# Where the operands of the MLP matmuls start within 256 bytes: padding the tiles of x, h and the last weights

## The chip, the cores and the metric

The kernel runs on one core of a Trainium2 chip. The metric is the time of one execution on the device in microseconds (us), the median of several runs. In the names below TensorE is PE (its loading of a stationary operand is PEld), VectorE is DVE, ScalarE is ACT, GpSimd is POOL, and SyncE, which issues the DMAs, is SP.

## What is computed

Attention with mixed heads, then two MLPs one after the other, all in float32:

```
# q, k, v: (4, 12, 448, 64); w_pre, w_post: (12, 12)
scores = einsum('bhij,hg->bgij', scale * q @ k.T, w_pre)
attn   = softmax(scores);  attn = einsum('bhij,hg->bgij', attn, w_post)
x      = (attn @ v) as (1792, 768)
# two MLPs, 768 -> 2048 -> 768 each
h = x @ w_in;   g = where(h > 0, h, exp(min(h, 0)) - 1);  x   = g @ w_out
h = x @ w2_in;  r = maximum(h, 0);                        out = (r * r) @ w2_out
```

## The kernel before

The first 434 us are the attention, the rest the two MLPs; in the MLPs the 1792 tokens are taken in two halves of 896, and each half runs through four layers (w1i, w1o, w2i, w2o) one after the other.

Every product of the MLPs is made of three matmuls in a lower-precision float form: each operand is split into a high part (a copy rounded to that form) and a low part (what is left over), and `three` adds high by high, high by low and low by high into one PSUM bank. So each call of `three` is one matmul of line 587, one of line 588 and one of line 589, in this order, and the MLPs are a chain of these triples: 192 for each of the first three layers of a half, 224 for the last. All instructions stand in the order in which the code is written.

A matmul has a stationary operand (128 columns of it are loaded into the array, by a LDWEIGHTS that the trace shows as PEld) and a moving one, which is then streamed through. In the calls of `three` the second argument pair names the stationary parts and the third the moving ones.

- In the layers w1i, w1o and w2i the weights stand (`wh`, `wl`, 128 columns each time) and the activations move: 448 tokens of `xh`, `xl` (layers w1i, w2i) or of `hh`, `hl` (layer w1o).
- In the layer w2o it is the other way round: the activations stand (`hh`, `hl`, 128 tokens) and the weights move (`wh`, `wl`, 384 columns), since the output is to have tokens as rows.

The tiles: `two_parts` makes a high and a low tile for x (6 x 896 floats a partition) or h (16 x 896), in the right (`xp`) or left (`hp`) pool, with some room behind or ahead of the data. `Weights.part` makes the tiles `wh` and `wl` of 512 floats, of which 384 or 512 are used; those of the layer w2o, which has 384, begin `OFF` floats into the tile. The names `two_parts`, `OFF`, `hp` and `xp` carry the change. Which address a tile gets follows from the sizes of the tiles allocated before it in its pool.

Ahead of the matmuls ACT and DVE split weights and activations (lines 475 and 476, 628 and 629, 658 and 659), apply the activation functions (620 to 625), and in the first half also turn the weights from the words in which they come into float32.

Of the kernel before, what the change touches and what calls it, by code (L numbers as in the profile page):

```python
# [8 lines left out]
F32R = mybir.dt.float32r  # L9
# [11 lines left out]
JC, NJ = 4, 112  # L21
KC, FC = DM // 128, DFF // 128
WU = 512
OFF = 8
EXP_MIN, EXP_MAX = 2.0**-15, float.fromhex("0x1.dffffep+16")


# [373 lines left out]
class Weights:  # L401
# [64 lines left out]
    def part(self, engine=None):  # L466
# [4 lines left out]
        n = self.units[i][3]  # L471
        at = OFF * self.units[i][4]
        hi = self.pool.tile([128, WU], F32R, name="wh", bufs=4)[:, at : at + n]
# [31 lines left out]
def col(i):  # L505
    return slice(i * 128, (i + 1) * 128)


class Mlps:
# [17 lines left out]
    def two_parts(self, k, pool, name, at):  # L527

        n = k * 2 * S
        t = [pool.tile([128, n + 2 * OFF], F32R, name=f"{name}{a}", tag=f"{name}{a}") for a in "hl"]  # L530
        return [x[:, at : at + n].rearrange("p (k s) -> p k s", k=k) for x in t]


# [31 lines left out]
    def new_x(self, half):  # L565
        self.half, self.xraw = half, {}
        self.nx = self.two_parts(KC, self.xp, "x", OFF)

# [39 lines left out]
    def run(self):  # L608
        nc, weights, blocks = self.nc, self.weights, self.blocks
        self.hp = self.pool("hp", "left")  # L610
        for half in range(2):
            xh, xl = self.nx
            for m in range(2):
                hh, hl = self.two_parts(FC, self.hp, "h", m * OFF)
                pending = []

                def activate(p, f, bl, m=m, hh=hh, hl=hl):
                    u = g = self.tmp()
                    if m == 0:
                        nc.scalar.activation(u, p, AF.Relu, scale=-1.0)  # L620
                        nc.scalar.activation(u, u, AF.Exp, scale=-1.0)
                        nc.vector.scalar_tensor_tensor(g, u, -1.0, p, ALU.add, ALU.max)
                    else:
                        nc.scalar.activation(u, p, AF.Relu)  # L624
                        nc.vector.tensor_tensor(g, u, u, ALU.mult)  # L625

                    def rest():
                        nc.scalar.copy(hh[:, f, bl], g)
                        nc.vector.tensor_tensor(hl[:, f, bl], g, hh[:, f, bl].bitcast(F32), ALU.subtract)  # L629

                    pending.append(rest)

                def flush():
                    for rest in pending:
                        rest()
                    pending.clear()

                for f in range(FC):
                    if half == m == f == 0:
                        p = self.begun  # L640
                    else:
                        p = self.inner(xh, xl, flush)
                    for j, bl in enumerate(blocks):
                        activate(p[j], f, bl)
                flush()
                if m == 0:
                    xh, xl = self.two_parts(KC, self.xp, "x", OFF)
                    for o in range(KC):
                        p = [self.bank()[:, :S] for _ in blocks]
                        for f4 in range(4):  # L650
                            wh, wl = weights.next()
                            for j, bl in enumerate(blocks):
                                for i in range(4):
                                    f = 4 * f4 + i
                                    self.three(p[j], wh[:, col(i)], wl[:, col(i)], hh[:, f, bl], hl[:, f, bl],
                                               f == 0, f == FC - 1)
                        for j, bl in enumerate(blocks):
                            nc.scalar.copy(xh[:, o, bl], p[j])
                            nc.vector.tensor_tensor(xl[:, o, bl], p[j], xh[:, o, bl].bitcast(F32), ALU.subtract)
                    continue  # L660
                n2 = DM // 2
                for nh in range(2):
                    p = [self.bank()[:, :n2] for _ in range(7)]
                    for f in range(FC):
                        if half == 0 and nh == 0:
                            if f == 0:
                                self.new_x(1)
                            if f < 12:
                                self.load_x(f)
                            if 2 <= f < 14:  # L670
                                self.split_x(f - 2)
                        wh, wl = weights.next()
                        for i in range(7):
                            self.three(p[i], hh[:, f, col(i)], hl[:, f, col(i)], wh[:, :n2], wl[:, :n2],
                                       f == 0, f == FC - 1)
                    for i in range(7):
                        o = self.tmp()[:, :n2]
                        if i % 2:
                            nc.scalar.copy(o, p[i])
                        else:  # L680
                            nc.vector.tensor_copy(o, p[i])
                        r = half * 2 * S + i * 128
                        nc.sync.dma_start(out=self.out[r : r + 128, nh * n2 : (nh + 1) * n2], in_=o)
# [49 lines left out]
```

## Time and profile before

| | |
|---|---|
| median of 3 runs | 1380.01 us (1379.79 to 1380.43) |
| the profiled execution | 1380.93 us |
| its span, first to last instruction | 1379.2 us |
| PE, share of the span | 99% |
| DVE, ACT, POOL | 62%, 49%, 19% |
| mean granted TensorE clock | 0.998 |
| attention / MLPs, from the start | 0 to 434 us / 434 to 1379 us |

The span is what the trace covers; 1.7 us of the profiled execution's time lie around it. Matmuls are pipelined: one starts while the one before is still on its way through the array, so the duration of one matmul in the trace is longer than the distance from its start to the start of the next, and the ends are modelled. The distance between starts is what adds up to time.

### The profile page before, as it was taken

To read this page: it belongs to the slowest core of one execution; us is meant where nothing else is said; L and a number is where in the kernel's file an instruction comes from. 1 tells how busy PE (TensorE), PEld (TensorE's weight loads), DVE (VectorE), ACT (ScalarE), POOL (GpSimd) and SP (SyncE) were. 2 spreads that over 40 slices of the span, in tenths; PEclk is the share of its full clock that TensorE was granted. 3 is DMA by queue.
4 is the path that set the end of the run, shared out by engine and by line. 5 is a ranking of instruction groups with operands and counts; after the bars stand their busy time and mean duration, and the time that the engine had idled before them with its cause. 6 is when DMAs were issued, how large, how long until landed. Compare 5 with 4: busy or idle time off the path is not lost.

```text
span 1379.2 us, 24203 instructions
## 1 busy us (share of the span) xinstructions
PE 1368.0 (99%) x8908; PEld 1248.8 (91%) x8908; DVE 860.7 (62%) x1928; ACT 669.1 (49%) x1502; POOL 265.3 (19%) x247
## 2 busy tenths in 40 slices
PE   7999999999999999999999999999999999999998
PEld 5888888888888999999999999999999999999998
DVE  6877778777886999866699996634442113443121
ACT  5776767776766677422355543235541113333111
POOL 3765655674656000000000000000000000000000
PEclk9999999999999999999999999999999999999999
DMA  5633633733644655545355575532121111211131
GB/s 157 200 107 126 204 106 124 206 120 117 199 141 127 197 172 172 187 153 175 125 162 163 170 253 179 175 99 58 52 79 54 47 46 46 58 52 58 41 109 40
DMA packets 104842, 174.40 MB, mean 126 GB/s; under 512 B 22707, under 2 KB 82195, under 8 KB 104723
## 3 DMA queue, kind: packets, MB, share of 16 engines
q1 hardware_dynamic: 104723, 172.85, 39.9%
q8 instruction: 70, 1.15, 0.4%
q14 instruction: 49, 0.40, 0.1%
HBM read 97.93 MB, written 36.18 MB: 97 GB/s over the span
## 4 chain that ended last, share of the span: by engine, by line
PE 97%; DVE 1%; issue 0%; DMA 0%; SPq 0%; POOL 0%; ACT 0%; ACTq 0%; DVEq 0%; POOLq 0%
PE ps_post L221 12%; PE ps_qk L588 11%; PE ps_qk L589 11%; PE ps_qk L587 11%; PE ps_qk L246 6%; PE ps_mix L588 6%; PE ps_post L588 6%; PE ps_mix L589 6%; PE ps_post L589 6%; PE ps_mix L587 6%; PE ps_post L587 6%; PE ps_qk L163 4%; PE ps_mix L192 3%; PE ps_mix L190 3%; PE ps_mix L191 2%
## 5 line engine op out<-in xcount | busy, mean ns | idle before, releaser
L475 ACT CAST wh<-wf 128x384 fp32r<-128x384 f32 (+1 forms) x240 | 126.7, 532 | 267.5 <-DVE wf L461 116.1
L476 DVE TENSOR_TENSOR wl<-wf,wh 128x384 fp32r<-128x384 f32 (+1 forms) x238 | 137.5, 581 | 156.3 <-ACT wh L475 155.3
L184 POOL TENSOR_TENSOR gl<-graw,gh 120x448 fp32r<-120x448 f32 x178 | 201.3, 1152 | 146.2 <-ACT gh L179 140.8
L221 PEld LDWEIGHTS ps_post<-wg,ex 120*112 120x112 f32 x1440 | 156.1, 177 | 22.0 <-DVE tot L205 7.5
L221 PE MATMUL ps_post<-wg,ex 120*112 120x120 f32 x1440 | 173.0, 273 | 0.8 <-DVE at L228 0.6
L199 ACT ACTIVATE ex<-ps_mix,nmax 120x448 f32<-120x448 f32 x180 | 113.3, 637 | 113.3 <-DVE nmax L197 109.9
L588 PE MATMUL ps_qk<-xl,wh 128*128 128x448 f32 x384 | 141.0, 367 | 0.0
L589 PE MATMUL ps_qk<-xh,wl 128*128 128x448 f32 x384 | 140.7, 367 | 0.0
L587 PE MATMUL ps_qk<-xh,wh 128*128 128x448 f32 x384 | 139.4, 363 | 0.0
L197 DVE TENSOR_REDUCE nmax<-ps_mix 120x1 f32<-120x448 f32 x180 | 109.7, 622 | 42.3 <-PE ps_mix L192 41.8
L228 DVE COPY at<-ps_post 112x480 f32<-112x480 f32 x162 | 105.5, 651 | 10.0 <-PE ps_post L221 10.0
L179 ACT CAST gh<-graw 120x448 fp32r<-120x448 f32 x180 | 95.4, 593 | 1.7 <-DMA graw<-sc 1.7
L166 ACT COPY sc<-ps_qk 120x448 f32<-120x448 f32 x179 | 82.5, 557 | 8.1 <-PE ps_qk L163 8.1
L625 DVE TENSOR_TENSOR tmp<-tmp 128x448 f32<-128x448 f32 x64 | 39.9, 624 | 73.6 <-ACT tmp L624 73.6
L246 PEld LDWEIGHTS ps_qk<-at,v 112*64 112x64 f32 x1536 | 73.9, 137 | 11.3 <-ACT gh L179 6.2
L246 PE MATMUL ps_qk<-at,v 112*64 112x110 f32 (+2 forms) x1536 | 81.8, 262 | 0.0
L437 ACT ACTIVATE wf<-wd 128x384 f32<-128x384 f32 (+1 forms) x120 | 69.6, 580 | 17.9 <-DMA wd<-w1i 9.2
L587 PEld LDWEIGHTS ps_qk<-xh,wh 128*128 128x128 f32 x384 | 72.4, 188 | 6.4
L588 PEld LDWEIGHTS ps_qk<-xl,wh 128*128 128x128 f32 x384 | 72.0, 188 | 6.2
L589 PEld LDWEIGHTS ps_qk<-xh,wl 128*128 128x128 f32 x384 | 72.0, 188 | 5.2
L587 PE MATMUL ps_qk<-wh,hh 128*128 128x384 f32 x224 | 75.4, 336 | 0.0
L629 DVE TENSOR_TENSOR hl<-tmp,hh 128x448 fp32r<-128x448 f32 x128 | 74.2, 620 | 1.9 <-DMA w1if<-wf 1.5
(139 smaller groups left out, 3160.3 us busy)
## 6 DMA issues: line engine op xcount, KB each, us to landing
graw<-sc SPq DMA_DIRECT2D x180, 210.0 KB
wd<-w1i SPq DMA_DIRECT2D x32, 384.0 KB
wd<-w1o SPq DMA_DIRECT2D x24, 512.0 KB
wd<-w2i SPq DMA_DIRECT2D x32, 384.0 KB
wd<-w2o SPq DMA_DIRECT2D x32, 384.0 KB
w1if<-wf SPq DMA_DIRECT2D x32, 192.0 KB
w1of<-wf SPq DMA_DIRECT2D x24, 256.0 KB
w2if<-wf SPq DMA_DIRECT2D x32, 192.0 KB
```

Of the source, the lines that this page charges most:

```text
L179: nc.scalar.copy(hi, graw[t])
L184: engine.tensor_tensor(lo, graw.pop(t), parts[t][0].bitcast(F32), ALU.subtract)
L197: nc.vector.tensor_reduce(nmax, p, AX.X, ALU.max, negate=True)
L199: nc.scalar.activation(e[-1], p, AF.Exp, bias=nmax, scale=1.0, accum_out=tot[:, t % 2 : t % 2 + 1])
L221: nc.tensor.matmul(p[:, c, :], e[:, c * NJ : (c + 1) * NJ], w, start=True, stop=True)
L228: nc.vector.tensor_copy(o, p)
L246: nc.tensor.matmul(p[64 * a : 64 * a + 64, k, :w], vt[b, i][:, jc, g * D : (g + 1) * D], at[n][:, jc, 6 * i + g, :w], start=(jc == 0), sto ...
L475: nc.scalar.copy(hi, f)
L476: (engine or nc.vector).tensor_tensor(lo, f, hi.bitcast(F32), ALU.subtract)
L587: mm(p, wh, xh, start=first, stop=False)
L588: mm(p, wh, xl, start=False, stop=False)
L589: mm(p, wl, xh, start=False, stop=last)
```

## The change

Three things are changed in where data lie inside their tiles, nothing else. The constant `OFF` goes from 8 floats (32 bytes) to 40 (160 bytes); a second constant `STAND` of 24 floats (96 bytes) is used for the h tiles of the second MLP, which stand; and the room in each tile of x and h goes from 16 floats to 64, 192 bytes a tile more.

```
-OFF = 8
+OFF, STAND = 40, 24
...
     def two_parts(self, k, pool, name, at):
 
         n = k * 2 * S
-        t = [pool.tile([128, n + 2 * OFF], F32R, name=f"{name}{a}", tag=f"{name}{a}") for a in "hl"]
+        t = [pool.tile([128, n + 64], F32R, name=f"{name}{a}", tag=f"{name}{a}") for a in "hl"]
         return [x[:, at : at + n].rearrange("p (k s) -> p k s", k=k) for x in t]
...
             for m in range(2):
-                hh, hl = self.two_parts(FC, self.hp, "h", m * OFF)
+                hh, hl = self.two_parts(FC, self.hp, "h", m * STAND)
```

The constant `OFF` also stands in `new_x` and `run` (the x tiles) and in `Weights.part` (the tiles of w2o); these lines are not edited, but move with it. The addresses that the two built programs hold, as bytes past a multiple of 256, are the same for every matmul of a layer, because the operands step by 512 bytes (stationary) and 1792 or 1536 bytes (moving), all multiples of 256:

| layers | operand | before | now |
|---|---|---|---|
| w1i, w2i | moving `xh` / `xl` | 128 / 192 | 128 / 128 |
| w1o | moving `hh` / `hl` | 128 / 192 | 128 / 128 |
| w1i, w1o, w2i | stationary `wh`, `wl` | 96 | 224 |
| w2o | moving `wh`, `wl` | 128 | 128 |
| w2o | stationary `hh` / `hl` | 160 / 224 | 224 / 224 |
| MLPs | raw and temporary tiles `wd`, `wf`, `tmp` | 96 | 224 |

The tiles of the attention keep their addresses: among its 448-column matmuls, those of lines 190 to 192 have `gh` and `gl` moving at 192 and `pre_h` and `pre_l` standing at 96 and 64. On every engine the instructions of the two programs are the same and stand in the same order.

## Rows read from the trace of the kernel before

**Rows 1.** The page's busy shares, clock by slice and the chain by engine:

```profile
PE 1368.0 (99%) x8908; PEld 1248.8 (91%) x8908; DVE 860.7 (62%) x1928; ACT 669.1 (49%) x1502; POOL 265.3 (19%) x247
PEclk9999999999999999999999999999999999999999
PE 97%; DVE 1%; issue 0%; DMA 0%; SPq 0%; POOL 0%; ACT 0%; ACTq 0%; DVEq 0%; POOLq 0%
```

**Rows 2.** Busy time by stretch: attention, then layers of both halves.

```profile
core 0: us, PE busy (x) PEld busy (x) DVE busy (x) ACT busy (x) POOL busy (x), PEclk, DMA share, GB/s
0.00:434.00 434.00, 426.36 (x4003) 361.43 (x4004) 340.19 (x906) 304.51 (x776) 262.09 (x244) 0.99 0.48 149
435.00:556.00 121.00, 121.00 (x670) 111.74 (x669) 107.41 (x223) 78.97 (x158) 2.26 (x3) 1.00 0.56 177
557.00:673.00 116.00, 116.00 (x573) 107.15 (x572) 76.57 (x137) 35.67 (x63) 0.00 (x0) 1.00 0.51 164
674.00:790.00 116.00, 116.00 (x572) 107.17 (x571) 104.22 (x220) 60.53 (x126) 0.00 (x0) 1.00 0.50 157
791.00:906.00 115.00, 115.00 (x665) 114.98 (x664) 80.21 (x170) 39.66 (x79) 0.00 (x0) 1.00 0.58 186
...
1025.00:1141.00 116.00, 116.00 (x572) 107.18 (x571) 23.90 (x38) 21.42 (x39) 0.00 (x0) 1.00 0.17 50
```

**Rows 3.** Line 587's matmuls, layer w1o of each half: duration, first and last start.

```profile
engine op xcount: duration ns min/median/max, first and last start us, forms
L587 PE MATMUL ps_qk<-hh,wh x96: 361/363/364, 576.4 to 673.4; 128*128 128x448 f32 x96
L587 PE MATMUL ps_mix<-hh,wh x48: 362/362/364, 556.9 to 651.4; 128*128 128x448 f32 x48
...
L587 PE MATMUL ps_qk<-hh,wh x96: 361/363/364, 1024.7 to 1121.7; 128*128 128x448 f32 x96
...
L587 PE MATMUL ps_post<-hh,wh x48: 362/363/364, 1046.7 to 1141.3; 128*128 128x448 f32 x48
```

**Rows 4.** The same for line 587 in layer w2o, first half.

```profile
L587 PE MATMUL ps_mix<-wh,hh x64: 335/336/340, 791.1 to 906.6; 128*128 128x384 f32 x64
L587 PE MATMUL ps_post<-wh,hh x64: 335/336/337, 791.7 to 907.1; 128*128 128x384 f32 x64
```

**Rows 5.** PE's timeline in layer w1o: start, duration, both us.

```profile
599.58 0.36 PE L587 MATMUL ps_post<-hh,wh 128*128 128x448 f32 x1
599.78 0.37 PE L588 MATMUL ps_post<-hl,wh 128*128 128x448 f32 x1
599.99 0.37 PE L589 MATMUL ps_post<-hh,wl 128*128 128x448 f32 x1
600.19 0.36 PE L587 MATMUL ps_post<-hh,wh 128*128 128x448 f32 x1
```

**Rows 6.** Groups by line and shape over the span: busy us, mean ns of one.

```profile
L588 PE MATMUL ps_qk<-xl,wh 128*128 128x448 f32 x384 | 141.0, 367 | 0.0
L589 PE MATMUL ps_qk<-xh,wl 128*128 128x448 f32 x384 | 140.7, 367 | 0.0
L587 PE MATMUL ps_qk<-xh,wh 128*128 128x448 f32 x384 | 139.4, 363 | 0.0
L587 PE MATMUL ps_qk<-wh,hh 128*128 128x384 f32 x224 | 75.4, 336 | 0.0
L588 PE MATMUL ps_qk<-wl,hh 128*128 128x384 f32 x224 | 75.4, 336 | 0.0
L589 PE MATMUL ps_qk<-wh,hl 128*128 128x384 f32 x224 | 75.4, 336 | 0.0
```

**Rows 7.** The attention's 448-column mix matmuls: three of a timeline, then durations.

```profile
301.69 0.36 PE L190 MATMUL ps_mix<-gh,pre_l 120*120 120x448 f32 x1
301.89 0.36 PE L191 MATMUL ps_mix<-gh,pre_h 120*120 120x448 f32 x1
302.09 0.37 PE L192 MATMUL ps_mix<-gl,pre_h 120*120 120x448 f32 x1
...
L191 PE MATMUL ps_mix<-gh,pre_h x180: 358/363/576, 20.5 to 428.1; 120*120 120x448 f32 x180
L192 PE MATMUL ps_mix<-gl,pre_h x180: 362/367/575, 21.5 to 428.3; 120*120 120x448 f32 x180
```

**Rows 8.** The end of the program: last matmul, last eviction, all stores.

```profile
1375.30 0.34 PE L589 MATMUL ps_qk<-wh,hl 128*128 128x384 f32 x1
1375.73 0.56 DVE L681 COPY tmp<-ps_qk 128x384 f32<-128x384 f32 x1 [0.54 <-PE ps_qk L589]
...
L683 SPq DMA_DIRECT2D out<-tmp x28: 332/338/2063, 847.0 to 1376.3; - x28
```

## Prediction, written before the changed kernel ran

> **What bounds the kernel now.** I began with the page's busy shares and the chain of what ended last. PE is busy for 99% of the span, the chain runs through PE for 97% of it, and nothing else has more than 1%; the clock row is at its top in all 40 slices, the 2.4 GHz level [rows 1]. So the time is the sum of what the matmuls take, one after the other, and a change counts only if it alters the distance from one matmul's start to the next.
>
> Next come the stretches. In the MLP layers PE is busy for the whole of each stretch (116.00 of 116 us), while DVE is busy for 24 to 107 us and ACT for 21 to 79 [rows 2]. No layer waits for an operand. The pace is then read from the first and last start of line 587, which opens each triple. In layer w1o of the first half the first of its 192 starts is at 556.9 and the last at 673.4: 116.5 / 191 = 0.610 us a triple, 203.3 ns a matmul. In the second half it is 1024.7 to 1141.3, 116.6 us [rows 3], the same within the rounding of these rows. In layer w2o the 224 starts go from 791.1 to 907.1: 116.0 / 223 = 0.520 us a triple, 173.4 ns a matmul [rows 4].
>
> What should they take? The two shapes differ by 64 columns, and line 587's durations differ by 363 - 336 = 27 ns [rows 6], which is 64 columns at one a cycle of 2.4 GHz (26.7 ns). So streaming alone is 448 / 2.4 = 186.7 ns and 384 / 2.4 = 160.0 ns. What is left over per matmul is **16.6 ns in the 448-column layers and 13.4 ns in w2o**. These layers run the same triple, with the same number of columns loaded (128). The surplus differs by 3.2 ns, and the durations say where it lies. Lines 588 and 589 take 367 ns where 587 takes 363, in the 448-column layers alone; in w2o all three take 336 [rows 6].
>
> Three things can make this difference: the other engines' traffic, the number of columns, or where operands start. The first is out. Layer w1o of the first half runs beside 76.6 us of DVE, 35.7 us of ACT and a DMA share of 0.51, and that of the second half beside 23.9, 21.4 and 0.17 [rows 2], at the same pace. Nor can it be that 587 reloads the stationary part that 588 then uses, while the others change it: in w2o the triple repeats its stationary part in the same way, and there the lines are equal. Between columns and starts the profile doesn't decide by itself. The starts do differ: w2o moves everything from 128 and has its stationary parts at 160 and 224, while the other layers move from 128 and 192 with stationary parts at 96.
>
> **The change, part by part.** No instruction is added, removed or moved on any engine, so there are no new waits, and no queue is reordered. What is new are addresses.
>
> *Layers w1i, w1o, w2i.* There are 6 such layers of 576 matmuls, 3456 or 1152 triples. Low parts move from 128 instead of 192, and weights stand at 224 instead of 96. That brings them to a pair of starts that w2o holds already: there line 588 streams weights from 128 while `hl`, standing at 224, is loaded for line 589, and it takes 336 ns like its neighbours. I price this from two sides:
> - By durations: if 588 and 589 come down to 587's 363 ns, that is 2 x 4 ns x 1152 = 9.2 us.
> - By surplus: if the layers come to w2o's 13.4 ns, that is 3.2 ns x 3456 = 11.1 us.
>
> I take the middle, **10.1 us**. A lower price comes from the attention's mix matmuls, also 448 columns wide, with both parts alike (at 192) and stationary ones at 96 and 64. They start 0.20 us apart, 0.60 us a triple [rows 7] against 0.61 in w1o [rows 5]. With only two decimals that says somewhere from 0 to 10 ns a triple, 0 to 11.5 us. They load 120 columns instead of 128 and run beside a busier POOL, so I use them as a bound only. The other bound is the shortest record among them, 358 ns: if every 448-column matmul came to that, the gain would be (5 + 9 + 9) x 1152 = 26 us.
>
> *Layer w2o.* Its moving start stays at 128, and the high stationary part goes from 160 to 224, where the low one is. Lines 587 to 589 have equal durations although their stationary starts differ [rows 6], so I put it at 0. The bounds: 5 ns better, which is the gap from 363 to the 358 of the mix, or 4 ns worse, the step that 588 and 589 show elsewhere, both times 1344 matmuls: -6.7 to +5.4 us.
>
> *The other engines.* `wd`, `wf` and `tmp` shift by 128 bytes modulo 256, so the splitting on ACT and DVE and the DMAs read and write at other starts. No row shows that this matters to them, and I take 0. What covers it is room: in the fullest layer DVE has 107.4 us of work in 121, in the next 104.2 in 116 [rows 2]. A matmul stream 1.5% faster shortens 116 us to 114 and still leaves DVE 10 us. Without that cover, DVE would have to become 10% slower before PE waits for splits.
>
> *Attention and tail.* The first 434 us keep their addresses; the end, from the last matmul at 1375.3 over the last copy to the last store issued at 1376.3 and its landing [rows 8], is untouched. Both 0.
>
> The sum: 1380.93 us of the profiled execution less 10.1 is 1370.8. That execution lay 0.9 us above the median of 1380.01, so the median to expect is **1370 us**, 0.7% faster.
>
> The Trainium skill speaks against this. "TensorE: Matmul & The Clock Gate", section "Step-by-step: what each phase is for", says that PE has two independent read ports into SBUF, so that loading the next stationary operand takes nothing from the matmul that is streaming. By that rule starts could not matter, and the time would stay at 1380. The same page's section "Back-to-back issue gap" gives columns / 2.4 + 2.5 ns for an isolated warm matmul, as an estimate 189.2 and 162.5 ns here. The trace shows 203.3 and 173.4, so here each matmul pays about 11 to 14 ns that this formula doesn't hold, and the measurement decides.
>
> **The rivals.**
> - *No change (about 1380).* The 3.2 ns belong to the number of columns, or to the pattern of accumulating into one bank, and starts do nothing. For it: no row names an address, and 587 already does 363 ns while moving from 128, the start from which 589 is slow. Against it: nothing else differs inside a triple of the 448-column layers that doesn't also differ in w2o, and there the lines are equal. If surplus merely grew with columns, w2o's 13.4 would become 15.6 at 448, leaving 1.0 ns x 3456 = 3.5 us for starts, a time of 1376.5. Chance 0.17 for within 0.2%, about what a measurement of this kernel can tell from no change (1377.2 to 1382.8).
> - *Slower (about 1387).* A moving start of 128 against a stationary start of 224 is itself a bad pair over 448 columns. Line 589 shows that 128 alone doesn't protect: it moves from 128 and takes 367. Then line 587 goes from 363 to 367 (4 ns x 1152 = 4.6 us), 588 and 589 keep theirs, and w2o, now at 224 for all, pays up to half of its bound of 5.4: 1380 + 4.6 + 2.7 = 1387. It decides from a mean of 0.8 ns a matmul over the 3456 (2.8 us). Against it stands w2o's line 588, which has this pair and shows nothing. Chance 0.13.
> - *Much faster (1355 to 1361).* All lines reach the 358 ns of the shortest mix record: 1380 - 26 = 1354. Only some of those records are that short (the median of line 191 is 363), so it is a tail. Chance 0.07.
> - *Half of it (1374).* Only the low part's move to 128 counts and only line 588 comes down: 4 ns x 1152 = 4.6 us, 1375.4; or only 589 does, the same. Chance 0.14.
>
> **How the numbers follow.** The forecast itself, both slow lines down to the third (1366 to 1374), has 0.49. With half of it and much faster that makes 0.70 for faster by over 0.2%, 0.17 for the same, 0.13 for slower. The likeliest case's own range is 1366 to 1374. To leave out no more than 2 in 10, the range cuts off most of the slower case (0.13) and much faster (0.07) and keeps no change: 1361 to 1382.
>
> **What would show it.** If the forecast is right, lines 588 and 589 of the 448-column layers read about 363 ns, the first and last start of 587 in layer w1o lie 114.6 to 115.0 us apart instead of 116.5, w2o keeps 116.0, and the attention's end stays at 434 us. It is wrong in its mechanism if 588 and 589 stay at 367 while time falls elsewhere, for example in w2o or on line 587, and wrong altogether if all durations stay. It would also be wrong if PE shows idle time in the MLPs, which it doesn't now.

## The result, and the profile after

The changed kernel takes 1368.26 us (median of 4 runs, 1367.12 to 1369.38) against 1380.1 us: a ratio of 0.9915, 95% interval 0.9904 to 0.9927, 0.85% faster. The profiled execution took 1367.75 us with a span of 1366.0, and its clock was 0.998 as before.

The busy shares of the page after, then the busy time by stretch, with the columns of [rows 2]:

```profile
PE 1355.9 (99%) x8908; PEld 1247.1 (91%) x8908; DVE 859.9 (63%) x1928; ACT 668.6 (49%) x1502; POOL 265.3 (19%) x247
...
0.00:432.00 432.00, 425.48 (x4002) 360.24 (x4003) 339.96 (x906) 304.29 (x775) 261.95 (x244) 1.00 0.48 150
554.00:668.00 114.00, 114.00 (x572) 106.98 (x571) 76.03 (x137) 35.13 (x63) 0.00 (x0) 1.00 0.51 166
669.00:783.00 114.00, 114.00 (x572) 106.98 (x571) 104.38 (x220) 60.20 (x126) 0.00 (x0) 1.00 0.52 160
1016.00:1130.00 114.00, 114.00 (x572) 106.98 (x570) 23.88 (x38) 21.11 (x39) 0.00 (x0) 1.00 0.17 51
```

PE is still never idle in the MLPs, and the work of the other engines is the same to within 1 us over the span. Only the distance between matmuls is new. Line 587's matmuls after, in layer w1o of both halves and in w2o of the first (duration min/median/max, first and last start, as in [rows 3, 4]), and one group each of lines 588 and 589 in w1o:

```profile
L587 PE MATMUL ps_qk<-hh,wh x96: 362/362/363, 572.5 to 667.9; 128*128 128x448 f32 x96
L587 PE MATMUL ps_mix<-hh,wh x48: 362/362/363, 553.3 to 646.3; 128*128 128x448 f32 x48
...
L587 PE MATMUL ps_qk<-hh,wh x96: 362/362/363, 1015.4 to 1110.8; 128*128 128x448 f32 x96
L587 PE MATMUL ps_post<-hh,wh x48: 362/362/363, 1037.0 to 1130.0; 128*128 128x448 f32 x48
...
L587 PE MATMUL ps_mix<-wh,hh x64: 335/336/336, 783.7 to 899.2; 128*128 128x384 f32 x64
L587 PE MATMUL ps_post<-wh,hh x64: 336/336/336, 784.2 to 899.7; 128*128 128x384 f32 x64
...
L588 PE MATMUL ps_qk<-hl,wh x96: 362/362/363, 572.7 to 668.1; 128*128 128x448 f32 x96
L589 PE MATMUL ps_qk<-hh,wl x96: 362/362/363, 572.9 to 668.3; 128*128 128x448 f32 x96
```

Layer w1o now goes from 553.3 to 667.9: 114.6 / 191 = 0.600 us a triple, 200.0 ns a matmul, against 203.3 of [rows 3], and all three lines have the same duration, which before they had not [rows 6]. Layer w2o keeps its 116.0 us and 173.4 ns. So each 448-column matmul now has the 13.3 ns above streaming that w2o had before.

The first triple of the MLPs starts at 432.8 in this profile and the last at 1361.8; the MLPs' matmuls take 929.3 us against 940.6 before, 11.3 us less, and the two medians lie 11.8 us apart. The span fell by 13.2, because the MLPs also began 1.9 us earlier (432.8 against 434.7). That looks like scatter between executions and not like the change: in the profiles of the eleven experiments below, where the attention is again the same, they began between 433.0 and 434.5.

One place in the profile after doesn't fit the idea of a pair of starts with one pace. PE's timeline after, in the first triples of the MLPs and then after the attention's last value matmuls, which stand behind the first 36:

```profile
433.72 0.37 PE L588 MATMUL ps_mix<-xl,wh 128*128 128x448 f32 x1
433.92 0.37 PE L589 MATMUL ps_mix<-xh,wl 128*128 128x448 f32 x1
434.13 0.37 PE L587 MATMUL ps_mix<-xh,wh 128*128 128x448 f32 x1
434.34 0.37 PE L588 MATMUL ps_mix<-xl,wh 128*128 128x448 f32 x1
...
445.92 0.36 PE L587 MATMUL ps_qk<-xh,wh 128*128 128x448 f32 x1
446.12 0.36 PE L588 MATMUL ps_qk<-xl,wh 128*128 128x448 f32 x1
446.32 0.36 PE L589 MATMUL ps_qk<-xh,wl 128*128 128x448 f32 x1
```

The same tiles at the same starts run at 207 ns apart first (433.72 to 434.34 is three steps) and at 200 later. The experiments had to explain this too.

### The profile page after: what moved, and what is told of

It is laid out like the page before. It is cut to its first block, busy times and chain, and to the rows that moved or that the text cites. A ratio compares the mean times of both kernels' runs of the same rounds, so it can differ in the third digit from the quotient of the medians.

```text
span 1366.0 us, 24203 instructions
## 1 busy us (share of the span) xinstructions
PE 1355.9 (99%) x8908; PEld 1247.1 (91%) x8908; DVE 859.9 (63%) x1928; ACT 668.6 (49%) x1502; POOL 265.3 (19%) x247
## 4 chain that ended last, share of the span: by engine, by line
PE 97%; DVE 1%; issue 0%; SPq 0%; DMA 0%; POOL 0%; ACT 0%; ACTq 0%; DVEq 0%; POOLq 0%
PE ps_post L221 12%; PE ps_qk L587 11%; PE ps_qk L588 11%; PE ps_qk L589 11%; PE ps_qk L246 6%; PE ps_mix L587 6%; PE ps_post L587 6%; PE ps_post L588 6%; PE ps_mix L589 6%; PE ps_mix L588 6%; PE ps_post L589 6%; PE ps_qk L163 4%; PE ps_mix L192 3%; PE ps_mix L190 3%; PE ps_mix L191 3%
## 5 line engine op out<-in xcount | busy, mean ns | idle before, releaser
L246 PEld LDWEIGHTS ps_qk<-at,v 112*64 112x64 f32 x1536 | 73.8, 137 | 11.3 <-ACT gh L179 6.5
L589 PE MATMUL ps_qk<-wh,hl 128*128 128x384 f32 x224 | 75.3, 336 | 0.0
L588 PE MATMUL ps_qk<-wl,hh 128*128 128x384 f32 x224 | 75.3, 336 | 0.0
```

What stands on the lines that cost most here:

```text
L246: nc.tensor.matmul(p[64 * a : 64 * a + 64, k, :w], vt[b, i][:, jc, g * D : (g + 1) * D], at[n][:, jc, 6 * i + g, :w], start=(jc == 0), sto ...
L588: mm(p, wh, xl, start=False, stop=False)
L589: mm(p, wl, xh, start=False, stop=last)
```

## The experiments

All are edits of the changed kernel. They give each tile of x, h and the weights its own room by tables in place of `OFF` and `STAND`; a step of 1 in a table is 4 bytes, and 0 is 224 bytes past a multiple of 256 for x and the weights, 128 past for h. "Distance" is the stationary start less the moving start, modulo 256. In the change it is 224 - 128 = 96 everywhere; before it was 96 - 128 = 224 and 96 - 192 = 160 in the 448-column layers, and 32 and 96 in w2o. The code is shortened: an `X_AT` with one entry holds for all four layers that read x, and where a line with `-` is missing, the lines with `+` stand in place of the change's own.

**Each half of the change alone.** The theory of the prediction was that the pair of starts counts; rivals were the low part's start alone and the stationary start alone.

```
# low_alike_only: room of the weights by layer; x, h as in the change
 def w_at(half, name, i):
     if name == "w2o":
         return OFF, OFF
-    return 0, 0
+    a = 0 if name == "w1o" else 32
+    return a, a
# stationary_only: room of (high, low)
-X_AT = (40, 40)   H_AT = [(0, 0), (STAND, STAND)]
+X_AT = (40, 56)   H_AT = [(0, 16), (STAND, STAND)]
```

> Both parts of x and h move from 128 as in the change, but the weights of w1i and w2i stand at 96 as before; those of w1o, whose tiles have no room to shift, stand at 224 and are the control. If the start of the low part was the cause: all six 448-column layers at 200.0 ns a matmul, total as the change, 1368 us. If the stationary start was the cause: w1o at 200.0, the four layers w1i and w2i stay at 203.4, 4 x 576 x 3.4 ns = 7.8 us above the change, 1376 us. If it is the pair of starts that counts, something between, with line 588 (moved from 192 before) and line 589 apart.

> The other half of the change alone: weights stand at 224 everywhere, but the low parts move from 192 (high parts 128) as before. If the low part's start was the cause: line 588 at 204 ns, and 589 too if it pays for the change of start, 1152 x 4 to 1152 x 9 ns = 4.6 to 10.4 us above the change, 1373 to 1379 us. If the stationary start was the cause: 200.0 on all lines, 1368 us.

Measured: low parts alone 1381.69 us, ratio to the kernel before 1.0012 (1.0003 to 1.0021); stationary parts alone 1387.97 us, 1.0057 (1.0045 to 1.0070). Neither half gains anything, and both are slower than before. Neither total lies where a reading above put it. Line 587 with low parts alone, in w2i of the first half, w1i of the second half and the control w1o of the first half, then with stationary parts alone, in w1o and in w2o:

```profile
L587 PE MATMUL ps_qk<-xh,wh x96: 369/369/369, 679.5 to 790.5; 128*128 128x448 f32 x96
L587 PE MATMUL ps_mix<-xh,wh x48: 363/369/369, 672.1 to 781.2; 128*128 128x448 f32 x48
...
L587 PE MATMUL ps_qk<-xh,wh x96: 363/363/363, 907.6 to 1017.4; 128*128 128x448 f32 x96
...
L587 PE MATMUL ps_post<-xh,wh x48: 363/363/363, 916.8 to 1024.8; 128*128 128x448 f32 x48
...
L587 PE MATMUL ps_qk<-hh,wh x96: 362/362/363, 576.1 to 671.5; 128*128 128x448 f32 x96
L587 PE MATMUL ps_mix<-hh,wh x48: 362/362/363, 556.9 to 649.9; 128*128 128x448 f32 x48
```

```profile
L587 PE MATMUL ps_qk<-hh,wh x96: 362/366/368, 576.3 to 673.8; 128*128 128x448 f32 x96
L587 PE MATMUL ps_mix<-hh,wh x48: 362/366/368, 556.7 to 651.8; 128*128 128x448 f32 x48
...
L587 PE MATMUL ps_mix<-wh,hh x64: 334/338/342, 792.2 to 909.9; 128*128 128x384 f32 x64
L587 PE MATMUL ps_post<-wh,hh x64: 337/340/342, 792.7 to 910.4; 128*128 128x384 f32 x64
```

With 128 against 96, w2i takes 672.1 to 790.5, 118.4 / 191 = 0.620 us a triple, 206.6 ns a matmul, while the control w1o is at 114.6 us. Layer w1i, with the same starts as w2i, takes 907.6 to 1024.8, 117.2 us or 204.4 ns a matmul: the same starts at two paces in one kernel. With 192 in the low part, w1o takes 117.1 us, 204.4 ns. Neither start alone brings 200.0 ns, so both single-start rivals fall. A new question comes from the last two lines: w2o has the same starts here as in the change, yet takes 118.2 us instead of 116.0, 176.7 ns instead of 173.4. Twice 2.2 us for w2o is over half of the 8 us by which the kernel with stationary parts alone is slower than the kernel before.

**The map of starts.**

```
# sweep_a: the four layers w1i, w2i (half 0), w1i, w2i (half 1)
+X_AT = {(0, 0): (40, 40), (0, 1): (40, 56), (1, 0): (56, 56), (1, 1): (8, 8)}
     if name == "w2o":
         return OFF, OFF
-    return 0, 0
+    a = 0 if name == "w1o" else 4 * (i // 2)   # i // 2: column block of h
+    return a, a
# sweep_b: the same with X_AT for moving starts 64, 96, 160, 224, parts alike
```

> A map, not a candidate. In w1i and w2i the stationary start goes through 0, 16, ... 240 from one of the 16 column blocks of h to the next; the moving starts (high/low) are 128/128, 128/192, 192/192 and 0/0 in the four such layers. If the stationary start alone counts: the same bad blocks in all four layers. If the moving start alone counts: each layer even over its blocks. If the pair counts: the bad blocks shift with the moving start. The pair 128 with 224 should give 200.0 ns and 128/192 with 96 should give 203.4, since those were seen.

> The same map for moving starts 64, 96, 160 and 224, both parts alike. Same readings as the other map. A pair below 200.0 ns (the change's pace, 13.3 ns above streaming) would mean that the surplus itself can be moved; if it is a fixed cost of each matmul, no pair goes below 200.0.

Measured: 1376.35 and 1381.22 us (one execution each). From the starts in the two traces I took, for every column block (36 matmuls at one pair of starts), the mean distance over ten triples. Seven layers with parts alike give seven visits to each distance, from seven moving starts:

| distance | ns a matmul | distance | ns a matmul |
|---|---|---|---|
| 0 | 202.67 (once 206.67) | 128 | 204.0 |
| 16 | 206.6 to 206.67 | 144 | 204.4 (once 200.00) |
| 32 | 204.4 (once 203.3) | 160 | 205.33 |
| 48 | 202.2 to 202.5 | 176 | 203.2 to 203.6 |
| 64 | 202.2 | 192 | **200.00** |
| 80 | 203.33 | 208 | 204.4 |
| **96** | **200.00** (once 206.67) | 224 | 206.67 |
| 112 | 204.0 | 240 | 203.3 |

So neither start counts by itself. With parts alike, the bad blocks wander with the moving start, and what remains is the distance modulo 256 bytes. Two cells of one layer show it, from PE's timeline of the first map, second half, w2i (moving from 0): distance 224, then 96:

```profile
1139.00 0.37 PE L587 MATMUL ps_qk<-xh,wh 128*128 128x448 f32 x1
...
1139.62 0.37 PE L587 MATMUL ps_qk<-xh,wh 128*128 128x448 f32 x1
...
1198.26 0.36 PE L587 MATMUL ps_qk<-xh,wh 128*128 128x448 f32 x1
...
1198.86 0.36 PE L587 MATMUL ps_qk<-xh,wh 128*128 128x448 f32 x1
```

The first triple takes 0.62 us, the second 0.60. The table also bears on the low-part kernel, which sits at 224: its w2i has the 206.67 ns of the table, but its w1i, at 204.4, does not. Nowhere is a mean below 200.00. But four visits were out of line with the six others at their distance, and all came first or shortly after a layer began, so after something else had run. One of them is the very first block, which has the change's own starts and was expected at 200.0.

The eighth layer of the maps, w2i of the first half in the first map, has unlike parts, moving from 128 and 192. Three of its blocks matter:

- With the weights at 96 it has the starts of the kernel before, and its triples settle at 203.3 ns a matmul, the pace of that kernel. The raw and temporary tiles stand where the change puts them, so their shift alone gains nothing here.
- With the weights at 224 it has the starts of the kernel with stationary parts alone, and takes 202.2 ns where that kernel took 204.4.
- With the weights at 176 its triples settle at 200.0 ns, with unlike parts; two starts of line 587 there, one triple apart:

```profile
768.14 0.36 PE L587 MATMUL ps_qk<-xh,wh 128*128 128x448 f32 x1
...
768.74 0.36 PE L587 MATMUL ps_qk<-xh,wh 128*128 128x448 f32 x1
```

**Unlike parts.** If the distance from a stream to the load beside it decides, unlike parts should do as well, as long as each load lies 96 past the stream it runs beside.

```
# unlike_matched: x from 128 / 192 (high / low)
+X_AT = (40, 56)
     if name == "w1o":
         return 0, 0
+    return 0, 16     # wh at 224, wl at 32; unlike_crossed: 16, 0
```

> In w1i and w2i the parts of x move from 128 and 192 as before the change, and the weights' parts stand at 224 (high) and 32 (low), so that each stationary load lies 96 bytes (modulo 256) past the stream that runs while it is loaded: wh for line 588 beside 587's stream from 128, wl for 589 beside 588's from 192, the next wh beside 589's from 128. All else as the change. If what counts is the distance from a stream to the load beside it: 200.0 ns on all lines in these layers, total as the change, 1368 us. If parts have to be alike, or a matmul's own two operands have to be 96 apart: 203 to 205 ns there, 7 to 12 us more.

> The same with the two weights' starts exchanged (wh at 32, wl at 224): the loads then lie 160, 32 and 160 past the streams beside them. In the maps these distances took 205.3 and 204.2 ns. If the distance from a stream to the load beside it counts: about 204 to 206 ns in w1i and w2i, 4 x 576 x 4 to 6 ns = 9 to 14 us above the change, 1377 to 1382 us. If only the set of starts in use counted, this and the matched kernel would be equal.

Measured: matched 1377.56 us (ratio 0.9980, 0.9971 to 0.9990), crossed 1382.32 (1.0018, 1.0008 to 1.0027). Line 587 in w2i of the first half, matched, then crossed:

```profile
L587 PE MATMUL ps_qk<-xh,wh x96: 363/367/370, 679.6 to 789.2; 128*128 128x448 f32 x96
L587 PE MATMUL ps_mix<-xh,wh x48: 362/367/368, 672.3 to 780.0; 128*128 128x448 f32 x48
```

```profile
L587 PE MATMUL ps_qk<-xh,wh x96: 368/368/368, 679.4 to 789.2; 128*128 128x448 f32 x96
L587 PE MATMUL ps_mix<-xh,wh x48: 367/368/368, 672.0 to 780.0; 128*128 128x448 f32 x48
```

The triples take 116.9 / 191 = 0.612 and 117.2 / 191 = 0.614 us: both are slow, and the matched one isn't at 0.600: 204.1 ns in all four of its layers. My refinement, that each load only has to be 96 past the stream beside it, didn't bring the fast pace. Unlike parts as such don't forbid it: the block of the first map at 176 was fast with them. Whether the matched starts have a fast pace that none of these four layers entered isn't shown. Nor do the totals tell the two kernels apart: 4.4 of the 4.8 us between them lie in w2o, which has the change's starts in both and took 118.2 us a half in the crossed kernel, 116.0 in the matched one. So the rival that only the set of starts in use counts stays open.

**What ran before.**

```
# kicks: weights of w1i and w2i at 96 but for every fourth column block
+    f = i // 2
+    if name == "w1o" or f % 4 != 3:
+        return 0, 0
+    q = 8 * half + 4 * (name == "w2i") + f // 4   # distance 16 * q
+    a = (4 * q - 24) % 64
+    return a, a
```

> The change, but in w1i and w2i every fourth column block of h has its weights at another start, so that each of 16 distances (0, 16, ... 240) comes once, followed by blocks at 96 again, and the last one of a layer is followed by a whole layer w1o or w2o at 96. If the pace follows from the distance alone: all blocks at 96 take 200.0 ns and w2o 173.3. If the pace also depends on what ran before (the same distance took 200.0 and 206.6 in the maps, and w2o 173.3 and 176.7): some kicks are followed by 206.6 (or 176.7 in w2o), and which ones is then known.

Measured: 1378.12 us (one execution). Blocks at 96 came out at 200.0 or at 206.67 ns, and nothing between. After blocks at 0, 16, 32, 64, 80, 112 to 192 and 208 the next stretch at 96 was fast; after 48, 224 and 240 it was slow. Layer w1o in the first half (after 48) and the second (after 176), then w2o in the first half (after 112) and the second (after 240):

```profile
L587 PE MATMUL ps_qk<-hh,wh x96: 367/367/368, 574.6 to 673.2; 128*128 128x448 f32 x96
L587 PE MATMUL ps_mix<-hh,wh x48: 363/367/368, 554.8 to 650.9; 128*128 128x448 f32 x48
...
L587 PE MATMUL ps_qk<-hh,wh x96: 362/362/363, 1022.3 to 1117.7; 128*128 128x448 f32 x96
L587 PE MATMUL ps_post<-hh,wh x48: 362/362/363, 1043.9 to 1136.9; 128*128 128x448 f32 x48
...
L587 PE MATMUL ps_mix<-wh,hh x64: 336/336/338, 790.1 to 905.6; 128*128 128x384 f32 x64
L587 PE MATMUL ps_post<-wh,hh x64: 336/336/336, 790.6 to 906.1; 128*128 128x384 f32 x64
...
L587 PE MATMUL ps_qk<-wh,hh x128: 337/340/342, 1254.0 to 1372.2; 128*128 128x384 f32 x128
```

The same tiles at the same starts take 118.4 us in one half and 114.6 in the other (w1o), 116.0 and 118.2 (w2o). So the distance 96 has **two paces**, and what ran before picks one, which then lasts: behind 36 matmuls at 48 the next 576 were slow, and so were the first three blocks of w2i after those. In the second map, w1i of the second half also ended at 48, and w1o behind it was slow as well, 206.7 ns. But the distance just ahead doesn't settle it: w2o was fast, at 173.3 ns, behind a layer at 224 in the kernel with low parts alone, and behind a block at 240 in the second map. Two paces at one distance fit the timeline at 433.72 above, and the w2o of the kernel with stationary parts alone. How the past picks the pace stays open.

**The map for w2o, and a long slow stretch.**

```
# sweep_w2o: moving start by row block of h
     if name == "w2o":
-        return OFF, OFF
+        a = 4 * (i % 16)
+        return a, a
```

> The change, but in w2o the moving start of the weights goes through 16 values from one row block of h to the next, the stationary start staying at 224: the map for 384 columns. If w2o was even before because of its distances (32 and 96): other distances now cost there as they do at 448 columns, up to 6 ns of 173. If it was even because of its 384 columns: all distances at 173.3.

Measured: 1383.02 us (one execution). The 384-column matmuls are as sensitive: 173.2 ns at distance 192, 173.5 at 32 and at 224, 175.0 at 208, 176.7 at 160, 179.4 at 16 (means over blocks of 21, the first steps after the switch included, worked out from the starts). So 384 columns don't protect by themselves. But their map is another: 0, 32, 144, 176, 192 and 224 all settle at 173.3 ns, though 32 and 224 took 204.4 and 206.7 at 448 columns. Of the fast distances of 448 columns, 192 is fast here too, and 96 was at its slow pace, 176.6, on all its visits. The last experiment below has one block of 448 columns with exactly w2o's starts of the kernel before: both parts moving from 128, the high stationary part at 160, the low one at 224. Two starts of line 587 there, two triples apart:

```profile
736.63 0.36 PE L587 MATMUL ps_qk<-xh,wh 128*128 128x448 f32 x1
...
737.85 0.36 PE L587 MATMUL ps_qk<-xh,wh 128*128 128x448 f32 x1
```

That is 1.22 us for six matmuls, 203.3 ns, on this one visit no better than the 448-column layers before the change. So w2o was even before because of its distances at its number of columns, not because of either alone. Behind the sweep all three 448-column layers of the second half run at the slow pace of 96. Line 587 in layer w1o, first half, then second:

```profile
L587 PE MATMUL ps_qk<-hh,wh x96: 362/362/363, 573.7 to 669.1; 128*128 128x448 f32 x96
L587 PE MATMUL ps_mix<-hh,wh x48: 362/362/363, 554.5 to 647.5; 128*128 128x448 f32 x48
...
L587 PE MATMUL ps_qk<-hh,wh x96: 367/367/368, 1021.7 to 1120.3; 128*128 128x448 f32 x96
...
L587 PE MATMUL ps_post<-hh,wh x48: 367/367/368, 1044.0 to 1140.1; 128*128 128x448 f32 x48
```

That is 114.6 against 118.4 us. Three such layers are 11.4 us, most of the 14.8 that this kernel lies above the change, with not a start altered in them.

**The other fast distance.**

```
# distance_192: x, h and w2o's weights move from 32, all stationary parts at 224
+X_AT = (16, 16)   H_AT = [(40, 40), (STAND, STAND)]   # w2o: return 16, 16
# distance_192_disturbed: the same, with w2o swept as above
```

> The change at another distance: all parts of x, h and of w2o's weights move from 32, all stationary parts at 224, so every load starts 192 past the stream beside it. In the maps this distance took 200.0 to 200.4 ns on each of its visits. If the pace follows from the distance and 192 has one pace only: 200.3 ns in all six 448-column layers, 1 us above the change, 1369 us. If 192 also has a second, slower pace that a long stay falls into: 203 to 207 ns, 1379 to 1391 us.

> The same with w2o's moving start swept over 16 values, as in the kernel that swept w2o: there the second half's three 448-column layers, at 96, came out at 206.67 ns after the sweep. If the pace left by the sweep is a second pace of the distance 96 alone: here the second half runs at 200.3 ns, and the total is the sum of 1369 and some 3 us for the swept w2o, 1372 us. If any distance can be caught in a slower pace: the second half at 203 ns or more, 1377 us or above.

Measured: 1367.96 us (ratio 0.9916, 0.9903 to 0.9930), and 1371.51 with the sweep (one execution). Lines 587 to 589 at distance 192, layer w1o of the second half; then line 587 there behind the sweep:

```profile
L587 PE MATMUL ps_qk<-hh,wh x96: 363/363/363, 1015.4 to 1110.8; 128*128 128x448 f32 x96
...
L588 PE MATMUL ps_qk<-hl,wh x96: 360/360/360, 1015.6 to 1111.0; 128*128 128x448 f32 x96
...
L589 PE MATMUL ps_qk<-hh,wl x96: 362/362/363, 1015.8 to 1111.2; 128*128 128x448 f32 x96
```

```profile
L587 PE MATMUL ps_qk<-hh,wh x96: 362/363/363, 1017.9 to 1113.3; 128*128 128x448 f32 x96
...
L587 PE MATMUL ps_post<-hh,wh x48: 362/362/363, 1039.5 to 1132.5; 128*128 128x448 f32 x48
```

At 192 the triple is at 0.600 us too, its lines no longer equal among themselves, and behind the same sweep it stays there: 1132.5 - 1017.9 = 114.6 us, where 96 took 118.4. No slow pace was seen at 192, whatever ran before.

**Is there something below 200 ns?**

```
# unlike_weights_map: wh and wl at two distances, one pair for each block
+    c = 32 * half + 16 * (name == "w2i") + i // 2
+    return (8 * (c % 8) - 24) % 64, (8 * (c // 8) - 24) % 64
```

> The change, but in w1i and w2i the high and the low part of the weights start at two different places: 8 by 8 distances from the stream (0, 32, ... 224 each), one pair for each column block of h. If 13.3 ns above streaming is a fixed cost of every matmul: no pair below 200.0 ns over a triple. If it is itself a collision that a better pair avoids: some pairs below 200.0. Pairs with both at 96 or both at 192 should give 200.0 to 200.3.

Measured: 1379.21 us (one execution). Of the 64 pairs, four stand at 200.00 ns over the triple (96/96, 192/192, and with unlike parts 96/0 and 192/32, high/low), none below, and the worst at 206.67. Each pair was visited once, so another pace of a pair would have gone unseen; w1o at 96, in the second half, was slow again (206.7 ns). Single lines go down to 196 ns, and another line of the triple gives it back. This is what a fixed cost of 13.3 ns a matmul would do; what that cost is, the runs don't say.

## Why the prediction was right

- *The stage and the quantity.* The time is the distance between matmuls in the 448-column layers, and no wait or other engine comes in: confirmed by stretches that are as full as before, with the gain lying there. The signs that the prediction named came out: 362 ns on all three lines, 114.6 us for w1o, 116.0 for w2o.
- *The size.* Two prices stood against each other, 9.2 us by durations and 11.1 by the surplus of w2o, and I took the middle, 10.1. The MLPs gave 11.3. The surplus was the better price, 3.3 ns instead of 3.2 over 3456 matmuls: durations left out that line 587 had something to lose as well. Its own duration only falls from 363 to 362, but in w1o of the first half the steps behind lines 587, 588 and 589 were 201.1, 204.2 and 204.7 ns, and all three are 200.0 now. w2o was put at 0 and stayed at its 116.0 us.
- *The other engines and the tail* were put at 0, and are. The attention's 1.9 us in the two profiles is scatter.
- *The cause was half right, and the rest was luck.* That starts make the surplus is right. The prediction took the new pair from w2o, where line 588 had it and showed nothing. But a pace does not carry over from 384 columns to 448: w2o's own starts took 203.3 ns in a block of 448 columns, 16.6 above streaming. And a pair of starts has no single pace: 96 has two. The change got the good one through what runs ahead of its layers, which no row of the profile before shows. In the rival that ended slower, the slow pace of 128 with 224 is real, 206.67 ns. Over all six layers it would have cost 3456 x 6.67 = 23 us against the fast pace, about 1391 us, more than the 1387 I gave. I had given it little by w2o's even lines, which show one of its two paces and only for 384 columns.
- *The rival "half of it"* was wrong in kind: each half alone is slower than the kernel before, by 0.1% and 0.6%, so the effects of the parts don't add. Both kernels have starts that take either of two paces (224 in one, w2o's 96 in the other), so their totals are no fixed price of either half.
- *The rival "columns"* (no change) falls by the result and by w2o's map: at other distances its 384 columns pay up to 6 ns too. But the columns are not idle: they decide which distances are fast.
- *The Trainium skill's rule* of two independent read ports ("TensorE: Matmul & The Clock Gate", "Step-by-step: what each phase is for") would have made starts irrelevant. The trace disagrees: in the maps the same instructions go from 200.00 to 206.67 ns when only the distance of the two operands' starts changes. Whether two reads meet, and where, stays open; in the matched kernel the distance between a stream and the one load beside it was not enough.

## What to carry to other kernels

Where TensorE is never idle, compare the distance between starts of like matmuls line by line: a few ns that differ by line and not by engine load point to where the operands start. Choose the distance between stationary and moving starts modulo 256 bytes rather than one of the two addresses, and map it for each number of columns in use: 224 is among the slowest at 448 columns and fast at 384. With the parts of an operand alike one number describes the choice; of the unlike settings tried, three reached 200.0 ns and most did not. Change the parts together, since half of such a change can cost more than it brings. Of two distances with the same time take the one that keeps its pace after a disturbance: here 192, at 1368.0 us, instead of 96, at 1368.3.

## What was not expected of the hardware

The pace of a matmul stream depended on what had run before it, at equal clock, equal addresses and without any wait: 200.00 or 206.67 ns for 448 columns at distance 96, 204.4 or 206.7 at distance 224, 173.3 or 176.7 for 384 columns at 96. The slow pace of 96 was kept through at least the 1728 matmuls of three layers. At the full clock level of 2.4 GHz, 200.00 and 173.33 ns are the columns and 32 cycles more. No setting here held a pace below that, and none shows what the 32 cycles are.
